# An attention and channel-mix kernel: the older rows are mixed into a buffer of their own, and one relu moves a step on

## Chip, cores and metric

One Trainium2 chip (trn2), one core of it. The time is the device time of one execution in microseconds; the runs shown are three of the kernel before, with their median. A trace is of one further execution, taken by the hardware profiler.

## What is computed

The reference first runs attention over 8 batches of 12 heads, 448 rows each, 64 columns a head, all in fp32, with scores that are capped by a tanh:

```python
scores = cap * np.tanh(scale * np.matmul(q, k.transpose(0, 1, 3, 2)) / cap)
attn = softmax(scores)                      # with 1e-9 added to the sum
x = np.matmul(attn, v)                      # heads side by side: 448 rows x 768 columns a batch
x_prev = x shifted down by one row, with a row of zeros ahead
xk = mu_k * x + (1.0 - mu_k) * x_prev
xr = mu_r * x + (1.0 - mu_r) * x_prev
k = np.maximum(xk @ w_k, 0.0)               # 768 x 1024
out = sigmoid(xr @ w_r) * ((k * k) @ w_v)   # 768 x 768 and 1024 x 768
```

## The kernel before, in words

Two heads make a pair, six pairs a batch, 48 pairs in all. The kernel goes through steps: step i computes the scores of pair i and, in the same step, later work of the pairs before it. Columns of x stand on the partitions (128 for a pair, so that hp = i % 6 is the pair's place among the 768) and rows along the free dimension. fp32 products are made from three fp32r products each (high x high, low x high, high x low), so every operand is split into a high and a low part.

What one pair goes through, by the names in the code:

- Step i: `scores` (lines 277 and 270, S0 to S3) on TensorE into one of two pairs of PSUM banks, `tanh` (line 290) and `exp` (line 303) on ScalarE, `red` (line 339) on VectorE, which sums the rows in blocks.
- Step i+1: `values` (V or W, lines 314 and 330) on TensorE into `pv`, one PSUM bank from a pool of two, so that the values of pair i+2 take the bank of pair i. `gather` (line 345) is four small DMAs that bring the sums of the four partition quarters together; `recip` (lines 349 to 356) adds and inverts them on VectorE; `rec_store` (line 359) writes them to DRAM; `rec_load` (line 368) reads them back, spread over the partitions, once they have landed.
- Step i+2: `norm` (line 372) multiplies `pv` by them into x on VectorE. `mix_old` (line 382) on ScalarE computes (1 - mu_k) times the row before. Before the change it writes this over the pair's own `pv` bank. `mix_new` (line 387) on VectorE adds mu_k times the row itself and writes `xk`. So the bank is in use until mix_new is done, and the values of pair i+2, in step i+3, wait for it. `x_high` and `x_low` (GpSimd, xkh and xkl) split xk; `gate_old` (line 405, GpSimd) and `gate_new` (line 399, VectorE) do the same mixing with mu_r, from SBUF alone.
- When a batch has its six pairs, its key matmuls (`K`, `krow` line 489 or `kpart` line 464, 144 positions a batch) are spread over the next batch's steps. They fill two PSUM banks; a bank that is finished goes on the list `done`, and `relu` (line 501, ScalarE) reads whatever stands on that list at this point of the program. `k_store` (ScalarE's queue) or `k_put` (SyncE's queue) writes it to DRAM. `turn` (line 496) is a tiny ScalarE copy out of a key bank that holds back the key matmuls behind it.

After step 49 the second phase follows (line 702): the two big products by a seven-product scheme, solid on TensorE.

The order of the work is written out by hand. A step's list of names is a string: `STEP_0`, `STEP_6`, `STEP_7`, `EVEN_6`, `ODD_6` for steps 0 to 11, `TURN` for 12 and 13, and for steps 14 to 47 `ROWS`, of which `rows(phase)` picks those names whose prefix holds the phase (i % 6), with the matmuls' part put in for `PE`, `PE_TURN` and `PE_END`; steps 48 and 49 have `LAST`. Each engine executes its own instructions in the order of the program. In phase 5 (steps 17, 23, 29, 35, 41, 47) the matmuls `S2 N0 K18` stand ahead of `tanh1 exp1 relu` in the program; N0 is the first scores of the next step's pair. K18 finishes no block there, except in step 47: the keys of batch 6 go over to the plain order at position 108 (`ROWS_LAST`), so its last 18 finish block 6 of batch 6, and the relu of that step has three blocks to read instead of two. The lines that set this:

```python
        self.xold = self.PV.pop(i)[:, 0:S]                     # 381, mix_old
        self.nc.scalar.mul(self.xold, self.X[i % 2][:, 0:S], self.om["k"][:, hp:hp + 1])
            self.PV[i] = self.ps_v.tile([P, 512], F32, name="pv")   # values; the pool has two
        for b, fc, ps in self.done:                            # relu
```

Of the kernel before, what the change touches and what calls it, by code (L numbers as in the profile page):

```python
# [10 lines left out]
F32 = mybir.dt.float32  # L11
# [6 lines left out]
B, H, S, D = 8, 12, 448, 64  # L18
# [6 lines left out]
NPAIR = B * NP  # L25
# [4 lines left out]
P = 128  # L30
# [28 lines left out]
ODD = """load_v gather quad_load weight_load S0 S1 V S2 red3 f f f f f gate_new tanh0 exp0 red0  # L59
# [2 lines left out]
weight_abs load_qk rec_load quad_load tail_open weight_store"""  # L62
EVEN = ODD.replace("V S2", "V S3 S2").replace(" red3", "").replace("tanh2", "tanh3 tanh2").replace("K relu k_store prep\n", "K exp3 red3 relu k_store prep\n")
ROWS = """load_v gather quad_load weight_load PE 135:red3 f f f f f gate_new tanh0 exp0 5:PE_TURN red0
weight_sum tanh1 exp1 14:PE_TURN 25:relu red1 norm recip x_store 14:k_put rec_store 25:k_put qk_high qk_low 2:mix_old 024:tanh3 tanh2 03:exp2 3:relu 01345:mix_old 0:relu mix_new x_high x_low gate_old
1245:exp2 red2 weight_rest weight_sum 024:exp3 024:red3 weight_abs load_qk rec_load quad_load weight_store PE_END"""
ROWS_PE = (("S1 V S3 S2 K18", "", "N0 N1 K15"), ("V", "turn S2 K15", ""), ("S0 S1 W K6 T S3 S2 K18", "", ""),
           ("S0 S1 V S2 K18", "", "N0 N1 K12"), ("V S3", "turn S2 K18", ""), ("S0 S1 V", "turn K6 S2 N0 K18", ""))
STEP_0 = """gather rec_load load_v x_store weight_load S0 S1 V0 S2 V1 S3 V2 V3 f f f f f tanh0 exp0 red0
weight_sum tanh1 exp1 weight_abs red1 recip rec_store qk_high qk_low tanh2 exp2 norm red2 tanh3 exp3 mix_old red3 mix_new x_high x_low  # L70
load_qk weight_store"""
ODD_6 = """load_v gather weight_load weight_low S0 S1 V S2 red3 f f f f f gate_new tanh0 exp0 red0 norm
weight_sum tanh1 exp1 K relu_early red1 tanh2 qk_rise relu exp2 mix_old k_store mix_new recip x_store rec_store qk_low x_high x_low gate_old
K red2 weight_rest weight_sum relu k_store K K weight_abs relu k_store load_qk rec_load weight_store"""
EVEN_6 = ODD_6.replace("V S2", "V S3 S2").replace(" red3", "").replace("tanh2 qk_rise", "tanh3 tanh2 qk_high").replace("weight_abs", "weight_abs exp3 red3")
# [6 lines left out]
TURN = (EVEN_6.replace("K K weight_abs", "K relu k_store weight_abs") + " N0 N1 K15",  # L82
        " ".join(x for x in ODD_6.replace("S0 S1 V S2", "V").replace("exp1", "exp1 turn S2 K15").split() if x not in ("K", "relu", "relu_early", "k_store")))
LAST = """gather f f f f V recip rec_store norm rec_load K mix_old relu k_store prep mix_new x_high x_low gate_old
K gate_new relu k_store prep K prep K relu k_store prep x_store tail_open"""
ALONE = 8
ROWS_LAST = 6 * NF * ND * 3 + 108


def rows(phase):  # L90
    pe = dict(zip(("PE", "PE_TURN", "PE_END"), ROWS_PE[phase]))
    do = [x.split(":") for x in ROWS.split()]
    return " ".join(pe.get(x[-1], x[-1]) for x in do if len(x) == 1 or str(phase) in x[0])


def strings(i):
    if i < ALONE:
        return ((STEP_0, STEP_0) if i < 6 else (STEP_6, STEP_7))[i % 2]
    if i < REST[0]:
        return (TURN if i >= 12 else (EVEN_6, ODD_6))[i % 2]  # L100
    if i < NPAIR:
        return rows(i % NP)
    return ((LAST, LAST) if i < NPAIR + 2 else (EVEN, ODD))[i % 2]


def f(ap):
# [3 lines left out]
class Body:  # L110
# [170 lines left out]
    def left(self, i):  # L281
        return (i,) if i < ALONE else (i, i + 1)

    def left_slots(self, i):
        return slice(i % 2, i % 2 + 1) if i < ALONE else slice(0, 2)

# [87 lines left out]
    def mix_old(self, i):  # L374
        b, hp = i // NP, i % NP
        if hp == 0:
            xh = self.xkp[b % 2].tile([P, ND, S], F32R, name="xkh", tag="xkh")
            xl = self.xkp[b % 2].tile([P, ND, S], F32R, name="xkl", tag="xkl")
            self.XK[b] = (xh, xl)

        self.xold = self.PV.pop(i)[:, 0:S]
        self.nc.scalar.mul(self.xold, self.X[i % 2][:, 0:S], self.om["k"][:, hp:hp + 1])

    def mix_new(self, i):
# [58 lines left out]
    def kpart(self, n0, n1):  # L443

        nc, per = self.nc, NF * ND * 3
        for n in range(n0, n1):
            b, r = divmod(n, per)
            if per <= n < ROWS_LAST:
                self.krow(b, r)
# [377 lines left out]
    def step(self, i, KS):  # L827

        nq = 0
        if self.maxima and i < NPAIR and i % 2 == 0:  # L830
            for j in (i, i + 1):
                self.row_maxima(j)
        pair = dict(load_qk=i + (3 if i < ALONE else 4), qk_high=i + 2, qk_low=i + 2, qk_rise=i + 2, load_v=i, S=i, tanh=i, exp=i, red=i)
        pair.update(dict.fromkeys("V W T gather recip rec_store".split(), i - 1))
        pair.update(dict.fromkeys("norm mix_old mix_new x_high x_low gate_old".split(), i - 2))
        pair.update(x_store=i - 3, gate_new=i - 3, N=i + 1)
        for op in strings(i).split():
            if op[0] == "K":
                n = self.k_next
# [11 lines left out]
            if op in pair:  # L851
                j = pair[op] if j is None else j
                if op == "load_qk" and i == ALONE:
                    self.load_qk(ALONE + 3)
                if i == NPAIR + 1 and op in ("x_high", "x_low"):
# [211 lines left out]
```

## Time and profile before

| | |
|---|---|
| runs, median (lowest to highest) | 906.75 us (906.21 to 907.01) |
| the profiled execution | 908.35 us |
| its span, first to last instruction | 906.5 us |
| TensorE (PE) busy | 874.6 us, 96% |
| VectorE (DVE) busy | 728.0 us, 80% |
| ScalarE (ACT) busy | 626.5 us, 69% |
| GpSimd (POOL) busy | 411.7 us, 45% |
| mean granted TensorE clock | 0.993 |
| the chain that ended last, by engine | PE 49%, DVE 25%, DMA 11%, ACT 5%, SPq 4% |

A line of the profile names the engine, the line of the kernel, the operation and its tiles as out<-in. SPq is SyncE's DMA queue, PEld the loading of weights. "[1.42 <-DVE xk L387]" behind an instruction says that its engine stood idle for 1.42 us before it, until the instruction of VectorE at line 387 that writes xk ended. PEclk is the granted share of the full TensorE clock: 1.00 is 2.4 GHz, 0.50 is 1.2 GHz. Matmuls follow one another in a pipeline, so a matmul's printed time overlaps the next one's. "x12" in a timeline is the number of instructions merged into one line.

### The profile page before, as it was taken

What the parts mean: (1) busy time and instruction counts of PE and PEld (TensorE: products, weight loads), DVE (VectorE), ACT (ScalarE), POOL (GpSimd) and SP (SyncE); (2) the same over time, 40 slices, a digit from 0 to 9 for tenths busy, and PEclk for the clock granted to TensorE, in tenths of its full rate; (3) what the DMA queues carried; (4) which work ended last, traced back from release to release, by engine and by line L of the source; (5) the groups of instructions that cost most, each with busy time, mean ns of one, the idle gap of its engine ahead of it and who ended that gap; (6) DMA issues with size and microseconds to landing.
All of it is one profiled execution on the core that took longest, in us unless ns stands there. A gap on an engine that the chain in (4) does not pass through costs nothing.

```text
span 906.5 us, 16778 instructions
## 1 busy us (share of the span) xinstructions
PE 874.6 (96%) x5826; PEld 705.4 (78%) x5826; DVE 728.0 (80%) x1246; ACT 626.5 (69%) x925; POOL 411.7 (45%) x345
## 2 busy tenths in 40 slices
PE   7889999999999999999999899999999999999997
PEld 3236666776667677766766699999999999999996
DVE  6888995988988899889868756887887667777775
ACT  8998887877788777878876365656565535555553
POOL 5996574777777777767763200000000024444330
PEclk9999999999999999999999999999999999999999
DMA  5465746677666776667565455745445546677663
GB/s 166 158 217 177 222 143 188 181 203 215 186 208 194 213 211 194 205 205 215 172 192 183 153 187 175 245 146 170 151 155 165 172 148 185 219 219 223 213 220 115
DMA packets 123679, 170.15 MB, mean 188 GB/s; under 512 B 22592, under 2 KB 107712, under 8 KB 123584
## 3 DMA queue, kind: packets, MB, share of 16 engines
q1 hardware_dynamic: 120992, 164.88, 59.4%
q10 hardware_dynamic: 2592, 4.10, 1.2%
q8 instruction: 48, 0.79, 0.4%
q14 instruction: 47, 0.39, 0.1%
HBM read 109.91 MB, written 56.60 MB: 184 GB/s over the span
## 4 chain that ended last, share of the span: by engine, by line
PE 49%; DVE 25%; DMA 11%; ACT 5%; SPq 4%; issue 3%; POOL 0%; DVEq 0%; ACTq 0%; POOLq 0%
PE ps L702 39%; DVE r L339 8%; DMA sq__195<-r 8%; PE kps L464 4%; SPq L345 4%; ACT p L290 2%; DVE wsq L568 2%; DVE wa L571 2%; DVE xk L387 2%; PE pv L314 2%; DVE wa L573 2%; ACT p L303 2%; DVE sq__195 L349 2%; DMA r<-rec_d 2%; PE s L277 1%
## 5 line engine op out<-in xcount | busy, mean ns | idle before, releaser
L290 ACT ACTIVATE p<-s,scl_t 128x896 f32<-128x896 f32 (+1 forms) x172 | 166.4, 979 | 31.6 <-PE s L270 17.4
L339 DVE TRANSPOSE_TENSOR_REDUCE r<-p 128x28 f32<-128x896 f32 (+1 forms) x192 | 180.2, 968 | 9.5 <-ACT p L303 9.0
L303 ACT ACTIVATE p<-p,cap_t 128x896 f32<-128x896 f32 (+1 forms) x172 | 175.0, 1024 | 4.6 <-ACT ko L501 0.4
L314 PE MATMUL pv<-p,rv 128*64 128x448 f32 x576 | 125.7, 565 | 18.6 <-DVE xk L387 18.4
L666 POOL TENSOR_TENSOR s<-src 128x384 f32<-128x384 f32 x14 | 14.3, 1021 | 266.4 <-DVE lo L687 266.4
L702 PE MATMUL ps<-wvh,hi 128*128 128x384 f32 x392 | 131.0, 334 | 0.0
L702 PE MATMUL ps<-wvl,hi 128*128 128x384 f32 x392 | 131.0, 334 | 0.0
L686 ACT CAST hi<-s 128x512 fp32r<-128x512 f32 (+1 forms) x112 | 63.6, 568 | 89.5 <-PE ps L702 76.8
L687 DVE TENSOR_TENSOR lo<-s,hi 128x512 fp32r<-128x512 f32 (+1 forms) x112 | 70.0, 625 | 59.2 <-ACT hi L686 43.4
L489 PE MATMUL kps<-xkh,wkh 64*128 64x448 f32 (+1 forms) x540 | 113.8, 369 | 0.0
L489 PE MATMUL kps<-xkh,wkl 64*128 64x448 f32 (+1 forms) x540 | 112.2, 362 | 0.0
L489 PE MATMUL kps<-xkl,wkh 64*128 64x448 f32 (+1 forms) x540 | 112.0, 362 | 0.0
L134 POOL TENSOR_TENSOR qkl<-rqk,qkh 128x896 fp32r<-128x896 f32 x47 | 100.5, 2139 | 10.2 <-ACT qkh L128 6.7
L314 PEld LDWEIGHTS pv<-p,rv 128*64 128x64 f32 x576 | 36.7, 138 | 81.6 <-issue 47.9
L702 PE MATMUL ps<-wrh,hi 128*128 128x384 f32 x294 | 98.9, 336 | 0.3 <-DVE o L725 0.3
L702 PE MATMUL ps<-wrl,hi 128*128 128x384 f32 x294 | 98.8, 336 | 0.0
L686 ACT CAST hi<-src 128x512 fp32r<-128x512 f32 (+1 forms) x84 | 47.7, 568 | 62.9 <-PE ps L702 59.9
L702 PE MATMUL ps<-wvh,lo 128*128 128x384 f32 x392 | 83.7, 334 | 0.0
L584 POOL TENSOR_TENSOR wsq<-wa,wsq 128x384 f32<-128x384 f32 (+1 forms) x40 | 54.2, 1354 | 60.7 <-DVE wsq L577 48.5
L687 DVE TENSOR_TENSOR lo<-src,hi 128x512 fp32r<-128x512 f32 (+1 forms) x84 | 56.8, 676 | 21.5 <-ACT hi L686 19.3
L702 PEld LDWEIGHTS ps<-wvh,hi 128*128 128x128 f32 x392 | 73.6, 188 | 0.1
L702 PEld LDWEIGHTS ps<-wvl,hi 128*128 128x128 f32 x392 | 73.6, 188 | 0.0
(118 smaller groups left out, 1920.3 us busy)
## 6 DMA issues: line engine op xcount, KB each, us to landing
rqk<-qk SPq DMA_DIRECT2D x47, 448.0 KB
src<-k_d SPq DMA_DIRECT2D x56, 256.0 KB
rv<-v SPq DMA_DIRECT2D x48, 256.0 KB
r<-rec_d SPq DMA_DIRECT2D x96, 112.0 KB
v_d<-o SPq DMA_DIRECT2D x56, 192.0 KB
src<-x_d SPq DMA_DIRECT2D x42, 256.0 KB
vl<-v_d SPq DMA_DIRECT2D x56, 192.0 KB
out<-o SPq DMA_DIRECT2D x55, 192.0 KB
```

The source lines that it names most:

```text
L134: {"p": self.nc.gpsimd, "v": self.nc.vector}[e].tensor_sub(*a)
L290: self.nc.scalar.activation(p32[:, n], self.S.pop((i, g))[:, n, 0:S], AF.Tanh, scale=self.scl_t)
L303: self.nc.scalar.activation(p32, p32, AF.Exp, scale=1.0 if self.maxima else self.cap_t)
L314: nc.tensor.matmul(pv[p, 0:S], v[:, g, h, :], ph[:, (h + i) % 2, :], start=(g == 0), stop=False)
L339: self.nc.vector.tensor_reduce(out=r1[:, 0:RM].rearrange("p (x g) -> p x g", g=3)[:, :, g] if g < 3 else r1[:, RM:RC], in_=p32.rearrange(" ...
L345: self.nc.sync.dma_start(self.sq[:, q % 2 * 2 + q // 2], self.r1[i % 2][32 * q:32 * q + 32])
L464: nc.tensor.matmul(self.kps[fc][:, 0:S], w, m[:, dc, :], start=first, stop=last)
L489: self.nc.tensor.matmul(self.kps[c][:, 0:S], w[p, dc, c * P:(c + 1) * P], m[p, dc, :], start=s == 0, stop=last or way == 2 and t == 2, ski ...
L584: {"p": self.nc.gpsimd, "v": self.nc.vector}[e].tensor_add(sq, f(a), sq)
L686: self.nc.scalar.copy(hi, x)
L687: self.nc.vector.tensor_sub(lo, x, f(hi))
L702: self.nc.tensor.matmul(o, a[:, c, :], w[:, c, :], start=first and k == 0, stop=last and k == len(todo) - 1, skip_group_check=True)
```

## The change

From pair 12 on (`ROWS_FIRST`), mix_old writes into a tile of its own in SBUF (`xold`, one buffer) instead of the pair's PSUM bank, so that the last reader of the bank is norm. In phase 5, the matmuls `S2 N0 K18` move in the program from behind `turn K6` to behind that step's relu; they stand in a new place called `PE_REST`. The relu of phase 5 so finds the two blocks that K6 finished on its list, and in step 47 the third block is left for a relu and a store that are put at the head of step 48.

```diff
-weight_sum tanh1 exp1 14:PE_TURN 25:relu red1 norm recip x_store 14:k_put rec_store 25:k_put qk_high qk_low 2:mix_old 024:tanh3 tanh2 03:exp2 3:relu 01345:mix_old 0:relu mix_new x_high x_low gate_old
-1245:exp2 red2 weight_rest weight_sum 024:exp3 024:red3 weight_abs load_qk rec_load quad_load weight_store PE_END"""
+weight_sum tanh1 exp1 14:PE_TURN 25:relu 5:PE_REST red1 norm recip x_store 14:k_put rec_store 25:k_put qk_high qk_low 2:mix_old 024:tanh3 tanh2 03:exp2 3:relu 01345:mix_old 0:relu mix_new x_high x_low gate_old
+1245:exp2 red2 weight_rest weight_sum 024:exp3 024:red3 weight_abs load_qk rec_load quad_load weight_store 03:PE_END"""
...
-           ("S0 S1 V S2 K18", "", "N0 N1 K12"), ("V S3", "turn S2 K18", ""), ("S0 S1 V", "turn K6 S2 N0 K18", ""))
+           ("S0 S1 V S2 K18", "", "N0 N1 K12"), ("V S3", "turn S2 K18", ""), ("S0 S1 V", "turn K6", "S2 N0 K18"))
...
+ROWS_FIRST = 12
...
-    pe = dict(zip(("PE", "PE_TURN", "PE_END"), ROWS_PE[phase]))
+    pe = dict(zip(("PE", "PE_TURN", "PE_REST" if phase == 5 else "PE_END"), ROWS_PE[phase]))
...
-    return ((LAST, LAST) if i < NPAIR + 2 else (EVEN, ODD))[i % 2]
+    return (("relu k_store " + LAST, LAST) if i < NPAIR + 2 else (EVEN, ODD))[i % 2]
...
         self.xold = self.PV.pop(i)[:, 0:S]
+        if i >= ROWS_FIRST:
+            self.xold = self.up.tile([P, S], F32, name="xold", bufs=1)
         self.nc.scalar.mul(self.xold, self.X[i % 2][:, 0:S], self.om["k"][:, hp:hp + 1])
```

## Rows read from the trace of the kernel before

**Rows 1.** Windows: length, busy PE, PEld, DVE, ACT, POOL, PEclk, DMA share, GB/s

```profile
155.00:480.00 325.00, 318.55 (x2639) 227.02 (x2637) 283.72 (x479) 264.27 (x336) 233.01 (x183) 1.00 0.68 201
...
505.00:545.00 40.00, 40.00 (x194) 33.89 (x191) 26.44 (x37) 21.98 (x36) 5.04 (x4) 0.96 0.53 175
545.00:907.00 362.00, 354.81 (x2046) 354.10 (x2044) 270.54 (x490) 194.92 (x377) 60.05 (x56) 1.00 0.58 182
```

**Rows 2.** Waits of PE, 155 to 505 us: total, times, longest

```profile
PE pv L314 <- DVE xk L387: 11.0, 12, 2.8
```

**Rows 3.** Waits of DVE, 155 to 505 us

```profile
DVE sq__195 L349 <- DMA sq__195<-r: 26.1, 26, 2.0
...
DVE r L339 <- ACT p L303: 4.9, 5, 1.7
```

**Rows 4.** Timeline of SyncE's queue: two rec_store, one step apart

```profile
302.91 0.33 SPq L359 DMA_DIRECT2D rec_d<-rs  x1
...
313.47 0.34 SPq L359 DMA_DIRECT2D rec_d<-rs  x1
```

**Rows 5.** Timeline of ACT in steps 47 and 48: start, us, engine, line

```profile
490.36 0.64 ACT L382 ACTIVATE pv<-x,om_k 128x448 f32<-128x448 f32 x1 [2.72 <-DVE x L372]
...
494.76 0.14 ACT L496 COPY turned<-kps 128x1 f32<-128x1 f32 x1
...
496.80 0.96 ACT L501 ACTIVATE ko<-kps 128x448 f32<-128x448 f32 x2
501.32 0.54 ACT L501 ACTIVATE ko<-kps 128x448 f32<-128x448 f32 x1 [3.56 <-PE kps L464]
...
503.20 1.04 ACT L303 ACTIVATE p<-p,cap_t 128x896 f32<-128x896 f32 x1
511.67 0.64 ACT L382 ACTIVATE pv<-x,om_k 128x448 f32<-128x448 f32 x1 [7.42 <-DVE x L372]
```

**Rows 6.** Timeline of DVE: norm, mix_new of pair 45; mix_new 46; xkl 47

```profile
498.62 0.58 DVE L372 TENSOR_TENSOR x<-pv,r 128x448 f32<-128x448 f32 x1
...
503.32 0.68 DVE L387 SCALAR_TENSOR_TENSOR xk<-x,mu_k,pv 128x448 f32<-128x448 f32 x1 [1.81 <-ACT pv L382]
...
512.41 0.68 DVE L387 SCALAR_TENSOR_TENSOR xk<-x,mu_k,pv 128x448 f32<-128x448 f32 x1 [0.78 <-ACT pv L382]
...
520.53 0.63 DVE L134 TENSOR_TENSOR xkl<-xk,xkh 128x448 fp32r<-128x448 f32 x1 [0.63 <-ACT xkh L128]
```

**Rows 7.** Timeline of PE: values of pair 46, last keys, values of pair 47

```profile
492.75 2.48 PE L314 MATMUL pv<-p,rv 128*64 128x448 f32 x12 [1.42 <-DVE xk L387]
...
497.38 0.47 PE L464 MATMUL kps<-xkh,wkh 128*128 128x448 f32 x1
...
504.05 4.17 PE L314 MATMUL pv<-p,rv 128*64 128x448 f32 x12 [2.77 <-DVE xk L387]
```

**Rows 8.** Windows around the two waits of rows 7, columns as rows 1

```profile
490.00:497.00 7.00, 5.58 (x44) 3.27 (x40) 5.32 (x11) 6.58 (x9) 3.10 (x3) 1.00 0.46 156
...
505.00:506.00 1.00, 1.00 (x6) 0.44 (x4) 1.00 (x2) 0.00 (x0) 1.00 (x2) 0.50 0.48 158
```

**Rows 9.** Lines 387, 399, 382, 426 by themselves: ns least/median/most

```profile
L387 DVE SCALAR_TENSOR_TENSOR xk<-x,mu_k,pv x48: 626/627/682, 31.5 to 519.2; 128x448 f32<-128x448 f32 x48
...
L399 DVE SCALAR_TENSOR_TENSOR xg<-x,mu_r,xg x34: 661/679/1347, 160.0 to 513.0; 128x448 f32<-128x448 f32 x34
...
L382 ACT ACTIVATE pv<-x,om_k x48: 618/639/643, 30.1 to 518.5; 128x448 f32<-128x448 f32 x48
...
L426 ACT ACTIVATE xl<-xo,om_r x14: 657/659/672, 547.3 to 713.2; 128x448 f32<-128x448 f32 x14
```

**Rows 10.** Timeline of PE: first keys of the last batch on pairs 46, 47

```profile
517.77 0.37 PE L464 MATMUL kps<-xkh,wkh 128*128 128x448 f32 x1
...
523.97 0.37 PE L464 MATMUL kps<-xkh,wkh 128*128 128x448 f32 x1
```

**Rows 11.** Waits of POOL, 155 to 505 us

```profile
POOL xkh L124 <- DVE xk L387: 71.6, 34, 8.1
```

More of the change, by code (lines that the diff above doesn't have):

```diff
@@ L99, in strings @@
     if i < REST[0]:
-        return (TURN if i >= 12 else (EVEN_6, ODD_6))[i % 2]
+        return (TURN if i >= ROWS_FIRST else (EVEN_6, ODD_6))[i % 2]
     if i < NPAIR:
         return rows(i % NP)
-    return ((LAST, LAST) if i < NPAIR + 2 else (EVEN, ODD))[i % 2]
+    return (("relu k_store " + LAST, LAST) if i < NPAIR + 2 else (EVEN, ODD))[i % 2]
 def f(ap):
```

## The prediction, made before the changed kernel ran

> **What bounds the kernel now.** I read the busy times by stretch first. From 155 to 480 us, the steady steps of attention, TensorE is busy 318.55 of 325 us at full clock, so it looks like the bound; from 505 to 545 it has no gap at all, and behind that it is busy for 354.81 of the 361.5 us left, the last outputs included [rows 1]. Then the waits: between 155 and 505 us TensorE stood idle for one reason only, the values' matmuls waiting for mix_new: 12 times, 11.0 us [rows 2]. That wait is what the change takes away, and the naive sum is 11 us.
>
> So the next question is what sets the pace of mix_new. The waits of VectorE in the same stretch name no TensorE instruction: 26 waits, 26.1 us, are for the gather's DMA and 5, 4.9 us, for an exp [rows 3]. The queue of SyncE shows why: rec_store is issued at 302.91 and the next one at 313.47, 10.56 us later, about one step, and in between the queue runs rec_store, rec_load (which waits for rec_store to land), a few other transfers, the gather, and then recip waits for the gather to land [rows 4]. This ring (recip, rec_store, rec_load, gather, recip) has no matmul in it. The stretch of 350 us holds 350 / 10.56 = 33 such rounds, and mix_new, right behind recip in VectorE's order, keeps their pace. TensorE is about 11.0 / 33 = 0.33 us a step faster than the ring, and the wait on mix_new is where it gives that back. Freed at norm, the bank lets TensorE run ahead of the ring, but only once: norm of a pair stands between recip of the pair before and the two reductions in VectorE's order, so it has the ring's pace too. What TensorE gains in the steady steps it will lose again in front of norm, of tanh's banks or of the `turn`. I therefore count a gain only where TensorE ends a stretch that nothing else limits: in steps 47 and 48, after which TensorE is solid, so that what it gains there reaches the end [rows 1].
>
> **Steps 47 and 48, part by part.** In step 47 ScalarE's order is two relus, a third relu, tanh2, mix_old of pair 45, exp2. The third relu reads the key block that the step's last 18 key matmuls finish: ScalarE stands still for 3.56 us before it, until 501.32 [rows 5]. Only then come tanh2, mix_old and mix_new, for which VectorE waits 1.81 us, until 503.32 [rows 6]. The values of pair 47, first in step 48, need the bank of pair 45, so they start at 504.05, after 2.77 us idle: the key matmuls before them ended at 501.28 [rows 7]. After that wait the granted clock is 0.50, the lower level (1.2 GHz); in 490 to 497 it is 1.00 [rows 8]. These 12 matmuls take 4.17 us, the same 12 of pair 46 take 2.48: 1.69 us more [rows 7].
>
> The change takes both causes away. The bank of pair 45 is free when norm ends, 498.62 + 0.58 = 499.20 [rows 6], 2.1 us before TensorE wants it at 501.28. The relu of the third block moves behind exp2; then tanh2 runs at 497.8 (behind the two relus, 496.80 + 0.96), mix_old at 499.2 (norm's end) for 0.64 us and exp2 for 1.04 us, to about 500.9 [rows 5], so the third part of the values, which starts some 1.6 us into them, finds its operand. **Gain: 2.77 us of idle and 1.69 us of slow clock, 4.46 us**, if the 18 key matmuls end when they do now. They will: the first waits for the first relu of step 47 (ready at 496.80 + 0.54, start 497.38), which ScalarE reaches by mix_old of pair 44 at 490.36, after a wait for norm of 2.72 us, and then exp, tanh and `turn` in a row [rows 5, 7]. That is the ring again, so nothing upstream of it moves them.
>
> The other edits. **Order of step 17, 23, ... 47:** the matmuls of `S2 N0 K18` keep their order on TensorE, and the relus before them keep theirs on ScalarE; only the list that relu works off changes, and only in step 47 are there three blocks. Cost nothing in the other steps. In step 47 SyncE puts two key blocks instead of three, and in step 48 ScalarE issues one more relu (0.54 us) and one store, where it waits 7.42 us for norm anyway [rows 5].
>
> **mix_new from SBUF:** with a PSUM input it takes 627 ns, the same operation with two SBUF inputs (the gate's mix) 679 ns in the median [rows 9]. Below, the price is nothing; above, 1347 - 627 = 720 ns, the longest of those rows. I take 52 ns, since the median is of the same shape and in the same steps. It lies beside the DMA wait in 26 steps and on the ring in 33 - 26 = 7: 0.36 us. **mix_old into SBUF:** 659 against 639 ns for the same form [rows 9], on the path only where VectorE waits for an exp that follows mix_old, 5 times [rows 3]: 0.10 us. Its new buffer is single, but the mix_new that empties it lies a step back.
>
> **What is late next:** the key matmuls of the last batch. Those that need pair 46 start at 517.77, those that need pair 47 at 523.97 [rows 10]. Shifted by 4.46 us that is 513.31 and 519.51. mix_new of pair 46 ends at 512.41 + 0.68 = 513.09, xkl of pair 47 at 520.53 + 0.63 = 521.16 [rows 6]. Their chain moves by up to 1.81 us, what mix_new of pair 45 no longer waits: that leaves 2.0 us for xkh and xkl of pair 46, and xkl of pair 47 is ready at 519.35, so nothing waits. If the chain did not move, xkl of pair 47, which the third matmul reads (two spacings of 0.2 us later, 519.92), would be 1.24 us late. Between 0 and 1.24, I take 0.2, since the wait that held the chain goes altogether.
>
> **Sum:** -4.46 + 0.36 + 0.10 + 0.20 = -3.80 us. The profiled execution took 908.35 us, 1.85 more than its span of 906.5; it becomes 904.55. It stands 1.60 us over the median of the runs, 906.75, so against those the forecast is 902.95 us. About 0.2% of the time, 1.8 us, is what a measurement of this kernel tells from no change.
>
> **Rivals.**
> *The idle time moves and takes the clock along* (17%). The values of pair 46 wait 1.42 us now and start at 492.75 [rows 7]. Freed at norm of pair 44 (just before mix_old, 490.36) they start some 2.4 us sooner and end near 492.8, but the key matmuls behind them wait for `turn`, which ends at 494.90 [rows 5]: about 2.1 us idle in one piece. After 1.42 us the clock held, after 2.77 us it fell [rows 7, 8]; 2.1 lies between. If it falls, some 1.2 of such 1.69 us are lost, as about 0.5 us of room lies before the 18 key matmuls: 904.1.
> *The values of pair 47 find another wait* (11%): their third part at exp2 (about 500.9), or their load. A part of the 2.77 us stays and the clock falls all the same: on average 1.4 us gained, 905.4.
> *TensorE was the bound after all* (9%). All 11.0 us come back [rows 2], with 1.69 of clock: 906.75 - 12.7 = 894.1. For it speaks that no other wait of TensorE is listed; against it, that VectorE waits for DMA 26 times and never for a matmul [rows 3].
> *Slower, by a port* (6%). mix_new gets its second input from SBUF while GpSimd reads there. Its rows of two SBUF inputs reach 1347 ns [rows 9], so a third of the steps at that price is 0.24 us a step, 33 x 0.24 = 7.9 on the ring: 906.75 + 7.9 - 4.5 = 910.2. It decides from 4.46 / 33 = 0.14 us a step. Against it: GpSimd stands idle before each xkh, 34 waits of 2.1 us in the mean, and what it waits for is mix_new itself [rows 11], so it hardly reads at that moment. The Trainium skill ("SBUF — State Buffer", Who interferes with whom) says that a VectorE instruction with two SBUF inputs contends with a GpSimd instruction that reads SBUF, while one with at most one SBUF input does not: by that rule this change moves mix_new into the contending kind. The long rows agree with it; no run before shows mix_new itself in that form.
> *The change doesn't free the bank at norm* (3%), and the values go on waiting for mix_new. With the relu gone from its way mix_new of pair 45 runs 1.81 us sooner [rows 6], and the values of pair 47 with it; 2.77 - 1.81 = 0.96 us stays idle, less than the 1.42 after which the clock held [rows 7, 8]: 1.81 + 1.69 - 0.66 of costs = 2.84 us gained, 903.9.
>
> **How the numbers follow.** The forecast has 54%; its own range is 902.0 to 903.9. Faster are the forecast, the moved idle time, the full gain and the bank that isn't freed: 0.54 + 0.17 + 0.09 + 0.03 = 0.83. Within 0.2% is the other wait: 0.11. Slower is the port: 0.06. The range goes from 900.5 (a ring that comes out 2 us quicker, as its DMA waits are not fixed) to 905.8, which takes in most of the case with another wait: 0.54 + 0.17 + 0.03 and most of 0.11, about 0.8.
>
> **What would show it.** Right: no wait of a value matmul on mix_new from pair 14 on, few on norm; ScalarE's third relu of step 47 behind exp2 without a wait of microseconds; the values of pair 47 directly behind the key matmuls, in 2.5 us at full clock; but rec_store to rec_store still about 10.5 us, so that mix_old of pair 44 comes within 1 us of 490.36 [rows 5] and TensorE's idle time in the steady steps stands before other instructions. Wrong: mix_old of pair 44 earlier by several us (then TensorE set the ring's pace), a mix_new of 1 us or more, or a stretch at the lower clock in step 47.

## The result, and the profile after

The changed kernel is slower: 911.5 us in the median of 12 runs against 906.38 of the kernel before beside it, ratio 1.0053, 95% interval 1.0028 to 1.0078, or +4.8 us (2.5 to 7.1). A second set of runs gave 1.0039 (1.0019 to 1.0058), +3.5 us. Single runs of either kernel lie up to 8.7 us apart, much wider than the three first shown, so times below are ratios to runs of the kernel before in the same set, given in us, and one profile alone settles nothing below some 3 us (an estimate from that spread). The profiled execution took 912.58 us with a span of 910.8.

Windows of the changed kernel, columns as in [rows 1]:

```profile
155.00:480.00 325.00, 321.36 (x2615) 223.11 (x2612) 283.75 (x480) 261.44 (x332) 231.33 (x183) 1.00 0.68 199
480.00:505.00 25.00, 23.03 (x178) 16.23 (x175) 20.43 (x29) 17.83 (x24) 8.80 (x7) 0.93 0.60 180
505.00:545.00 40.00, 38.45 (x190) 32.27 (x189) 27.65 (x37) 21.54 (x35) 6.51 (x5) 1.00 0.58 190
```

TensorE is busier in the steady steps than before (321.36 of 325 us against 318.55) and yet the trace counts fewer matmuls there (2615 against 2639). From 480 to 505 us its granted clock is 0.93, and from 505 to 545, where it had no gap, 1.55 us are idle. Its waits from 155 to 510 us:

```profile
PE kps L492 <- POOL xkl L135: 2.2, 6, 0.6
PE kps L492 <- ACT turned L499: 2.0, 1, 2.0
PE kps L492 <- ACT ko L504: 0.5, 1, 0.5
PE kps L492 <- POOL xkh L125: 0.3, 1, 0.3
```

The 11.0 us of waits on mix_new [rows 2] are gone, so the change does what it says. In their place stand short waits on GpSimd's xkl and ScalarE's relus, and one of 2.0 us on `turn`. VectorE waits for the gather as before, 26.4 us in 22 pieces against 26.1 in 26 [rows 3]. Its wait for the reciprocals from DRAM (r), 0.2 us in one piece before, is 1.4 us in three; that for xg was there before (6.0 us in 4):

```profile
DVE sq__195 L350 <- DMA sq__195<-r: 26.4, 22, 1.9
DVE r L340 <- ACT p L304: 6.1, 6, 1.7
DVE xg L402 <- POOL xg L408: 5.6, 4, 2.3
DVE x L373 <- DMA r<-rec_d: 1.4, 3, 0.6
```

The two mixes by themselves (ns least/median/most), which answer to [rows 9]:

```profile
L390 DVE SCALAR_TENSOR_TENSOR xk<-x,mu_k,xold x36: 629/631/684, 156.8 to 524.3; 128x448 f32<-128x448 f32 x36
...
L385 ACT ACTIVATE xold<-x,om_k x36: 659/670/673, 154.7 to 523.5; 128x448 f32<-128x448 f32 x36
```

In the median mix_new costs 4 ns more than from PSUM, mix_old 31 ns. Step 47 on TensorE (values of pair 46, then the 6 key matmuls, then the 18):

```profile
496.03 2.60 PE L315 MATMUL pv<-p,rv 128*64 128x448 f32 x12
500.60 0.74 PE L492 MATMUL kps<-xkh,wkh 64*128 64x448 f32 x2 [1.97 <-ACT turned L499]
501.14 0.57 PE L492 MATMUL kps<-xkh,wkl 64*128 64x448 f32 x2
...
508.00 1.35 PE L315 MATMUL pv<-p,rv 128*64 128x448 f32 x6
```

The values of pair 47 (508.00) stand directly behind the keys, as forecast; but 1.97 us of idle came up ahead of the 6 keys, and behind it a pair of matmuls takes 0.57 us where the same pairs took 0.36 or 0.37 before:

```profile
495.46 0.37 PE L489 MATMUL kps<-xkh,wkl 64*128 64x448 f32 x2
495.67 0.36 PE L489 MATMUL kps<-xkl,wkh 64*128 64x448 f32 x2
```

Three stretches part the loss. Up to norm of pair 12, which the change doesn't touch, the changed kernel took 154.00 us against 151.22; kernels with that same part took 150.8 to 155.6 in the profiles below, so this is spread. From norm of pair 12 to norm of pair 44 ("the steady stretch") it took 341.4 against 338.5 us, from there to the end of the span 415.4 against 416.8.

### The profile page after: what moved, and what is told of

It reads as the page before. It is cut to its first block, busy times and chain, and to the rows that moved or that the text cites. A ratio compares the mean times of both kernels' runs of the same rounds, so it can differ in the third digit from the quotient of the medians.

```text
span 910.8 us, 16779 instructions
## 1 busy us (share of the span) xinstructions
PE 879.0 (97%) x5826; PEld 704.7 (77%) x5826; DVE 730.6 (80%) x1246; ACT 626.4 (69%) x925; POOL 411.4 (45%) x345
## 4 chain that ended last, share of the span: by engine, by line
PE 49%; DVE 23%; DMA 12%; SPq 6%; ACT 4%; issue 3%; POOL 1%; DVEq 0%; POOLq 0%; ACTq 0%
PE ps L705 39%; DVE r L340 7%; DMA sq__195<-r 7%; SPq L346 5%; PE kps L467 4%; DMA r<-rec_d 3%; PE pv L315 2%; PE kps L492 2%; DVE xk L390 2%; DVE wsq L571 2%; DVE wa L574 2%; DVE sq__195 L350 2%; PE s L278 2%; DVE wa L576 2%; ACT p L291 2%
## 5 line engine op out<-in xcount | busy, mean ns | idle before, releaser
L492 PE MATMUL kps<-xkh,wkh 64*128 64x448 f32 (+1 forms) x540 | 116.9, 372 | 2.9 <-ACT turned L499 2.0
L492 PE MATMUL kps<-xkl,wkh 64*128 64x448 f32 (+1 forms) x540 | 114.2, 365 | 2.2 <-POOL xkl L135 2.2
L492 PE MATMUL kps<-xkh,wkl 64*128 64x448 f32 (+1 forms) x540 | 114.2, 364 | 0.0
L492 PEld LDWEIGHTS kps<-xkh,wkh 64*128 64x128 f32 (+1 forms) x540 | 64.0, 185 | 17.9 <-ACT turned L499 6.5
```

The source lines that it names most:

```text
L492: self.nc.tensor.matmul(self.kps[c][:, 0:S], w[p, dc, c * P:(c + 1) * P], m[p, dc, :], start=s == 0, stop=last or way == 2 and t == 2, ski ...
```

## The experiments

**The parts.** First each half of the change alone, the change for the last pairs alone, and the new tile alone:

```diff
# rows_only: the change, but steps 47 and 48 ordered as before (relu move undone)
# relu_only: the change without
-        if i >= ROWS_FIRST:
-            self.xold = self.up.tile([P, S], F32, name="xold", bufs=1)
# late_old:  if i >= 45:      tile_last: rows_only with  if i >= 47:
# rows_mid:  rows_only with  if 12 <= i < 44:
# all_but_44: the change with  if i >= 12 and i != 44:
```

> The changed kernel with the move of the third key block's relu undone: older rows mixed into SBUF from pair 12 on, steps 47 and 48 ordered as before. Theory U (using the SBUF rows lets TensorE run ahead and makes the steady steps 12 to 44 slower): the stretch from the first normalising that the change touches (pair 12) to that of pair 44 is 2 to 4 us longer than before, the first 150 us are as before within 1 us, and the time is +2 to +4 us. Theory P (the new tile moves the other tiles, whatever it is used for): the first 150 us are 2 to 3 us longer already and the time is +4 to +5 us. Theory N (the two profiles differ by chance): the time is within 1 us of before.

> The changed kernel with the older rows mixed into the values' PSUM bank for every pair, as before; only the relu of step 47's third key block is read in step 48. No new tile. Theories U and P: nothing is lost in steps 0 to 44; the idle of 2.8 us before the values of pair 47 shrinks since mix_old of pair 45 no longer stands behind three relus, so -2 to -4 us. Rival (the turn's relus bind step 47 wherever the third one stands): -1 to +1 us.

> The changed kernel, but the older rows go to SBUF only from pair 45 on; the relu is moved as in the change. Theory U: steps 12 to 44 are as before, TensorE is not ahead before the 6 key matmuls of step 47, so the whole forecast of the end comes, -2.5 to -4.5 us. Theory P: the tile is there, so the first 150 us are 2 to 3 us longer, and the time is 0 to -2 us. Theory N: -3 to -5 us, as the changed kernel would have it on average.

> The kernel before with the SBUF tile for older rows used by the last pair (47) alone, where nothing waits for the bank; no other edit. It has the layout of SBUF of the changed kernel and the order of before. Theory P: +2 to +5 us. Theories U and N: within 1 us of before.

| kernel | ratio to before (95%) | us | steady stretch, us |
|---|---|---|---|
| before (profile) | | | 338.5 |
| rows_only | 1.0031 (1.0008 to 1.0055) | +2.8 | 335.0 |
| relu_only | 0.9972 (0.9951 to 0.9994) | -2.5 | 334.3 |
| late_old | 0.9975 (0.9955 to 0.9995) | -2.3 | 333.9 |
| tile_last | 1.0003 (0.9985 to 1.0020) | +0.3 | 336.5 |

The tile alone costs nothing that can be measured (+0.3 us, -1.4 to 1.8), so theory P falls; theory N falls with it, since rows_only and relu_only differ from before by more than their intervals allow for chance. Theory U has the time of rows_only right, but not its profile, whose steady stretch is shorter than before's. The relu's move gains about what the end could give; late_old shows how, and what is lost again. Its TensorE in step 48 and the last batch's keys:

```profile
501.07 2.48 PE L316 MATMUL pv<-p,rv 128*64 128x448 f32 x12
...
511.75 0.47 PE L468 MATMUL kps<-xkh,wkh 128*128 128x448 f32 x1 [0.97 <-ACT ko L505]
```

and ScalarE, on which those keys wait:

```profile
510.60 0.67 ACT L386 ACTIVATE xold<-x,om_k 128x448 f32<-128x448 f32 x1 [8.87 <-DVE x L374]
511.17 0.52 ACT L505 ACTIVATE ko<-kps 128x448 f32<-128x448 f32 x1
...
519.16 2.31 ACT L821 CAST wvh<-w 128x768 fp32r<-128x768 f32 x3
521.37 1.57 ACT L821 CAST wvh<-wsq 128x768 fp32r<-128x768 f32 x2
522.84 1.57 ACT L821 CAST wvh<-w 128x768 fp32r<-128x768 f32 x2
524.31 0.83 ACT L821 CAST wvh<-wvl 128x768 fp32r<-128x768 f32 x1
525.04 0.98 ACT L505 ACTIVATE ko<-kps 128x448 f32<-128x448 f32 x2
```

The 12 value matmuls of pair 47 take 2.48 us behind the keys with no idle: the whole 4.46 us of the forecast. But the next key blocks need banks that a relu empties. One relu stands behind mix_old of pair 46, which waits 8.87 us for norm; the next behind eight casts of weights. TensorE, now earlier, waits 0.97 and 1.04 us for them; from 505 to 545 us it waits for nothing else:

```profile
PE kps L468 <- ACT ko L505: 2.0, 2, 1.0
```

From the values of pair 46 to the end of the span late_old takes 904.0 - 492.71 = 411.3 us, before 906.5 - 492.75 = 413.75: 2.45 us gained, 4.46 less these 2.01.

The rows of pairs 12 to 43 remained as the cost, and three more runs tested that:

> The changed kernel once more, unedited. Theory A (the two parts add up: rows +2.3 to +2.9 us, relu -2.3 to -2.5 us, as each alone measured): 0 to +1 us against the kernel before. Theory I (together they cost more than their sum, as the first twelve runs have it): +4 to +6 us.

> The kernel before with the older rows in SBUF for pairs 12 to 43 alone; pairs 44 to 47 and the relus as before, so the end has the order and the waits of before. Theory S (the cost of the rows lies in the steady steps): +2 to +3 us. Theory E (it lies in steps 45 to 48, where TensorE comes early to the 6 key matmuls and waits 2 us for the turn's copy): 0, within 1 us.

> The changed kernel with pair 44 alone mixed into its bank, so that the values of pair 46 wait for mix_new of pair 44 as before and TensorE is not early at the 6 key matmuls of step 47. Theory E: no wait for the turn's copy, no stretch of half clock in 480 to 505 us, rec_store of pair 44 to that of pair 47 29.4 us as in the kernel with the relu's move alone, and the time is 1 to 2 us below the changed kernel, -2 to -3 us against before if the rest is free. Theory S: the same at the end, but the steady steps cost 2 to 3 us: 0 to +1 us against before. Theory I: within 1 us of the changed kernel.

Measured: after_again 1.0039, +3.5 us; rows_mid 1.0040 (1.0022 to 1.0058), +3.6 us; all_but_44 1.0053 (1.0026 to 1.0080), +4.8 us. rows_mid has the end of the kernel before, so theory E falls and a loss of that size lies in the steady steps. all_but_44 took the wait for `turn` in step 47 away (0.2 us left from 480 to 505 us, granted clock 1.00 there) and gained nothing measurable, where theory S had 0 to +1 us against before. Theory A falls too: the rows alone (+2.8 or +3.6 us) and the end alone (-2.3 or -2.5 us) would make +0.3 to +1.3 us together, and the whole measured +3.5 (1.7 to 5.3) and +4.8. No run shows where the rest, some 3 us with an interval as wide, arises. The steady stretch is 335.0 to 342.9 us in the five profiles with rows in SBUF (mean 340.0) and 333.9 to 338.5 in the four without (mean 335.8): 4.2 us.

**Where in the steady steps.** I compared the five by the step's place in its cycle of six. The pairs 16, 22, 28, 34, 40 stand out. SyncE's queue there, changed kernel, pair 16:

```profile
188.82 0.34 SPq L360 DMA_DIRECT2D rec_d<-rs  x1
189.25 0.79 SPq L517 DMA_DIRECT2D k_d<-ko  x2
190.13 1.53 SPq L207 DMA_DIRECT2D rqk<-qk  x1
192.46 1.12 SPq L369 DMA_DIRECT2D r<-rec_d  x2
```

and before:

```profile
186.01 0.34 SPq L359 DMA_DIRECT2D rec_d<-rs  x1
186.44 0.79 SPq L514 DMA_DIRECT2D k_d<-ko  x2
187.33 0.41 SPq L206 DMA_DIRECT2D rqk<-qk  x1
187.83 2.08 SPq L368 DMA_DIRECT2D r<-rec_d  x2
```

In both one DMA's issue lasts some 1 us too long. Before, it is the second load of reciprocals; after, the load of queries ahead of them, so rec_load follows rec_store by 3.64 us instead of 1.82; 1.1 us of the difference is the issue, 0.7 a wait of SyncE until rec_store has landed. Over the five pairs the mean from rec_store to rec_load is 1.82 to 1.97 us in the four profiles without rows and 2.49 to 3.35 with them. What holds SyncE up shows in the DMA view of those microseconds (190.0 to 191.3 after):

```profile
q8 instruction: 1, 0.02, 6.0%
```

It is a fetch of instructions. Before, the whole stretch from 155 to 490 us has 22 of them, 16.4 KB each:

```profile
q8 instruction: 22, 0.36, 0.5%
```

At 20 of these 22 a DMA issue of SyncE lasts 0.5 to 1.1 us longer than its like. It holds the other way round as well: of SyncE's 419 DMA issues in this stretch 21 last over 0.4 us longer than the median of their kind, and 20 of them meet one of the 22 fetches (the other, at 463.46, meets a fetch of 8 KB on a second instruction queue, q14). Between the first and the last, 21 gaps, the trace has 5,373 instructions of TensorE, 5,312 of them matmuls and weight loads: 256 a gap in the mean. No other engine has more than 643 there. So it is TensorE's program that is fetched, one block every 256 instructions or 1.5 steps. The Trainium skill ("Runtime: NRT & Kernel Launch", Instruction fetch mechanics) states the same blocks of 16 KiB, 256 instructions, and calls their cost mostly hidden; for TensorE the trace agrees, since its waits from 155 to 505 us, 11.0 us, are all for mix_new [rows 2]; for SyncE's queue the measurement decides: 0.5 to 1.1 us at 20 of 22 fetches.

**Moving the fetch.** That made theory F: what counts is where in the ring's step the fetch falls. Matmuls of one column, put in steps 3 to 10 where TensorE waits anyway, shift all later fetches and nothing else that I know of:

```diff
+        for _ in range(PAD // 8 + (i - 3 < PAD % 8) if g == 1 and 3 <= i < 11 else 0):
+            nc.tensor.matmul(s[0:1, 0, S + 32:S + 33], self.mu["k"][:, 0:1], self.mu["k"][:, 0:1], start=True, stop=True)
         if g == 2:
             self.QK.pop(i)
```

> The kernel before with 12 one-column matmuls more (24 instructions of TensorE) in steps 3 to 10, into unused columns of a score bank; nothing else. Theory F (a fetch of TensorE's code, 16 KB about every 256 of its instructions, holds up SP's DMA issue for about 1 us, and what counts is where in the step it falls): every later fetch falls 24 instructions, some 1.2 us, earlier in the step, so that of steps 16, 22, 28, 34, 40 falls on the key stores or the load of queries ahead of rec_load, as in the changed kernel; rec_store to rec_load of these pairs goes from 1.9 to about 2.8 us and the time to +2 to +4 us. Theory R (it is TensorE's running ahead or the SBUF operand itself): within 1 us of before.

> The changed kernel with 112 such matmuls (224 instructions) in steps 3 to 10: every later fetch falls 32 instructions, some 1.6 us, later in the step. Theory F: the fetch of steps 16, 22, 28, 34, 40 falls on or behind rec_load, rec_store to rec_load there goes from 2.9 back to 1.9 us, and the time to between -1 and +2 us against before, 2 to 4 us below the changed kernel. Theory R: +4 us against before, as the changed kernel.

> The changed kernel with 32 such matmuls (64 instructions): every later fetch falls some 3.3 us earlier. Theory F: the fetch of steps 16, 22, 28, 34, 40 falls where SP waits for the reciprocals and holds up nothing there, rec_store to rec_load 1.9 us; the fetches of the steps between move to just ahead of a gather, where they may hold it up: -3 to +1 us against the changed kernel. Theory R: as the changed kernel, within 1 us.

> The kernel with the relu's move alone (-2.5 us) and the 112 matmuls. Theory F: the fetches fall 1.6 us later, that of steps 16, 22, 28, 34, 40 behind rec_load and ahead of the next gather, -1 to -4 us against before. Theory R: -2.5 us, as without them.

> The changed kernel with 56 one-column matmuls. The trace of the run before showed that each counts four instructions of TensorE (two loads, two matmuls), so these are 224, and every later fetch falls 32 instructions, some 1.6 us, later: that of steps 16, 22, 28, 34, 40 from 6.4-7.4 us behind the gather to 8-9 us, where the kernel before has it (7.3-8.1) or a little behind. Theory F: rec_store to rec_load of these pairs 1.9 us, the stretch from the normalising of pair 12 to that of pair 44 within 334 to 338 us as in the kernels that keep the bank, -2 to +1 us against before. Theory R (the loss is not the fetch's): +4 us.

> The kernel before with 6 such matmuls, 24 instructions, so that every later fetch falls 1.2 us earlier, the fetch of those five steps at 6.1-6.9 us behind the gather, where the changed kernel has it. Theory F: rec_store to rec_load of these pairs 2.6 to 3 us and +2 to +5 us against before. Theory R: within 1 us of before.

Each such matmul turned out to be two loads and two matmuls, so the first four shifted twice as far as meant. Measured: before_pad12 +5.3 us (3.3 to 7.4), after_pad112 +1.1 (-0.5 to 2.6), after_pad32 +4.2 (2.8 to 5.6), relu_pad112 +0.8 (-0.9 to 2.6) against -2.5 without, after_pad56 +3.1 (1.4 to 4.9), before_pad6 +1.2 (-0.4 to 2.7). The nine kernels with added matmuls, of this part and the next, reach norm of pair 12 after 150.6 to 152.9 us, no later than those without, so the matmuls by themselves cost no time that shows. The same 112 matmuls make one kernel faster and another slower, which theory R has no place for. But of F's ranges only that of after_pad112 held clearly: before_pad12, relu_pad112 and after_pad56 came out above theirs, before_pad6 below, and after_pad32 fits both theories. The detail, too, came out otherwise than F had it: in before_pad6 the fetch of the five steps did not move (7.5 to 8.2 us behind the gather in four of them, as before), and after_pad56 and after_pad32 had rec_load back at 1.8 us and lost elsewhere, in the steps whose gather or rec_store now met a fetch. A fetch put ahead of rec_load is at most one place that costs, not the only one. The next run bears on this:

```diff
-... weight_abs load_qk rec_load quad_load ...
+... weight_abs 01234:load_qk rec_load 5:load_qk quad_load ...
```

> The changed kernel with the load of queries behind rec_load in the steps of phase 5 (those that bring back the reciprocals of pairs 16, 22, 28, 34, 40); the fetch stays where it is in TensorE's program. Theory F: a fetch that fell on the load of queries no longer holds up rec_load, rec_store to rec_load of these pairs from 2.9 to 1.8-2.3 us; what it then holds up is the next gather, so 0.5 to 2.5 us below the changed kernel. Theory R: as the changed kernel, within 1 us.

1.0079 (1.0054 to 1.0105), +7.1 us: rec_store to rec_load fell to 1.96 us as expected, and the time did not fall (the changed kernel had +4.8 and +3.5 us). Those five rounds of the ring got longer (11.56 us from rec_store to the next against 10.99 in the mean of the kernels with rows), because from the next gather to its reciprocals 6.19 us went by instead of 5.42. The load of queries now stands between rec_load and that gather; that it is what holds the gather up is not shown.

**The operand, the running ahead, and four positions.** The last four runs part the causes. rows_held is rows_mid with one more instruction: the rows of pairs 12 to 43 lie in SBUF, but VectorE clears a column of the bank behind mix_new, so TensorE waits as before:

```diff
+        if self.held is not None:
+            self.nc.vector.memset(self.held[:, 0:1], 0.0)
```

> The kernel before with the older rows in SBUF for pairs 12 to 43, but the values' bank held as before: VectorE clears one column of it (128x1) right behind mix_new, so the next values wait for that. Theory F (TensorE running ahead moves its fetches and small waits against the ring of reciprocals): rec_store to rec_load of pairs 16, 22, 28, 34, 40 1.8 to 2.0 us as before, and the time 0 to +2.5 us, what is above 0 being the 32 clearings. Theory O (the SBUF operand itself slows the steady steps): as with the bank freed, +3.6 us and the clearings on top, +4 to +6 us.

> The kernel before with 32 one-column matmuls in steps 3 to 10 (128 instructions of TensorE): the partner of the changed kernel with the same 32. Theory F (the change costs by where the fetches fall; with the fetches moved it costs another amount, of either sign): this one lies anywhere from -3 to +6 us against before, so that the changed kernel less this one is not +4 us in each of the four pairs (0, 32, 56, 112 matmuls) and lies within 2 us of 0 in the mean. Theory S (rows in SBUF cost 3 to 4 us in the steady steps wherever the fetches fall): this one is within 1.5 us of before, and the changed kernel 3 to 5 us above it.

> The kernel before with 56 such matmuls (224 instructions): partner of the changed kernel with 56. Theories F and S as for 32: F -3 to +6 us against before, S within 1.5 us of before.

> The kernel before with 112 such matmuls (448 instructions): partner of the changed kernel with 112 (+1 us against before). Theory F: +1 to +5 us against before (the relu's move alone lost 3 us by these 112). Theory S: -3 to -1 us, that is 3 to 4 us below the changed kernel with 112.

rows_held: 0.9997 (0.9980 to 1.0013), -0.3 us; rec_store to rec_load of the five pairs 1.83 us. TensorE waits for the cleared column, and the clearings are short:

```profile
PE pv L315 <- DVE pv L394: 3.1, 5, 0.8
PE pv L315 <- DVE xk L391: 2.8, 1, 2.8
```

```profile
L394 DVE MEMSET pv<- 128x1 f32 x32 | 1.9, 59 | 0.0
```

So the operand in SBUF costs nothing that can be measured; theory O falls. What costs 3.6 us in rows_mid is the freed bank alone, that is TensorE running ahead. And whether the change costs depends on the matmuls added, that is on where the fetches fall if F is right:

| matmuls added | before | changed | difference |
|---|---|---|---|
| 0 | 0 | +4.8, +3.5 | +4.1 |
| 32 | +6.8 (4.5 to 9.2) | +4.2 | -2.6 |
| 56 | +8.0 (5.2 to 10.9) | +3.1 | -4.9 |
| 112 | +4.2 (2.6 to 5.8) | +1.1 | -3.1 |

(us against the kernel before as it is; each from its own ratio. From the intervals, the differences with matmuls are known to about 2.7, 3.3 and 2.2 us, an estimate, so that of 32 is just not told apart from nothing.) With matmuls added the change gains 2.6 to 4.9 us; as the kernel stands, it loses 4.1. The mean of the four is -1.6, within F's 2 us of 0. Theory S of these runs falls: it had the kernel before within 1.5 us of itself with 32 and 56 matmuls. F had these two at no more than +6 us, and they came out above. The profile of before_pad56 is of its fastest run (905.67 us), so no trace shows where its 8.0 us go.

The gain isn't the rows'. With 112 matmuls the relu's move alone stands 3.4 us below the kernel before (+0.8 against +4.2) and the rows on top of it add 0.3 (+1.1); with 32 and 56 the two were not measured apart. So the freed bank costs some 4 us as the kernel stands and nothing that can be measured with 112 matmuls, and no pair shows that it gains. With none added the kernel before is at the fastest of the six positions tried (0, 6, 12, 32, 56 and 112 matmuls; 6 not told apart from 0).

## Why the prediction was wrong

*Steady steps: no gain, +0.46 us of costs.* Right that the 11.0 us are no reserve: no steady stretch got below 333.0 us in any of the kernels, and mix_old of pair 44 came 5.6 us later in the changed kernel's profile, not sooner (2.8 us of it from before pair 12). Right too, and too high, on mix_new's price (4 ns in the median, not 52) and near on mix_old's (31 ns, not 20). Wrong was the step "a gain only where TensorE ends a stretch that nothing else limits", with running ahead counted at nothing: it let TensorE gain or hold, never lose. In its place the runs showed that running ahead is an edit of its own. With the bank freed the steady steps cost some 4 us (rows_mid +3.6, steady stretch +4.2), and with the same operand but the bank held nothing (rows_held -0.3). What carries that cost is shown in part: TensorE's place against SyncE's queue shifts, and with it the fetches that hold that queue up. The trace of before had the sign of it, and my working left it out: 22 fetches in the DMA view, and at 298.85 a DMA issue of SyncE of 1.40 us whose like took 0.53 at 310.64, while I took the ring's pace from one round [rows 4].

*Steps 47 and 48: -4.46 us.* The mechanism was right, and late_old shows it: values of pair 47 behind the keys without idle, in the 2.48 us of full clock. In the changed kernel's profile the end, from norm of pair 44 on, gained 1.3 us. *What is late next*, +0.20 us, was the term mis-sized: it measured 2.01 us in late_old (1.4 us in the changed kernel). I followed xkh and xkl of the last pairs, but not the relus that empty the key banks; behind an engine said to be solid I had not asked which of its operands had time to spare only because it was late. The end alone is worth -2.3 to -2.5 us.

*The rivals.* "The idle time moves and takes the clock along" came true in the changed kernel: 1.97 us before the 6 keys, then matmuls at the lower clock (0.57 us a pair). Its price was small: all_but_44, without it, is no faster. That the values of pair 47 find another wait did not happen.

"Slower, by a port", the only one on the side where the result fell, came near the measured time by luck (+3.5 us forecast). Its mechanism is in the trace, but hardly any of the time. The Trainium skill ("SBUF — State Buffer", Who interferes with whom) has a VectorE instruction with two SBUF inputs contend with a GpSimd instruction that reads SBUF. The trace agrees: of the 36 executions of mix_new with both inputs in SBUF ten met GpSimd's splitting of the queries (qkl), and the seven that met it for 156 to 181 ns took 640 to 660 ns, the rest 629 to 632 ns but for the last two (683 and 684 ns, with no GpSimd beside them). Before, with one input in PSUM, seven met it for 159 to 178 ns and took 626 or 627 ns. One meeting of each, first in the changed kernel, then before:

```profile
378.47 2.14 POOL L135 TENSOR_TENSOR qkl<-rqk,qkh 128x896 fp32r<-128x896 f32 x1
380.43 0.66 DVE L390 SCALAR_TENSOR_TENSOR xk<-x,mu_k,xold 128x448 f32<-128x448 f32 x1
```

```profile
373.07 2.13 POOL L134 TENSOR_TENSOR qkl<-rqk,qkh 128x896 fp32r<-128x896 f32 x1
375.03 0.63 DVE L387 SCALAR_TENSOR_TENSOR xk<-x,mu_k,pv 128x448 f32<-128x448 f32 x1
```

Over the whole kernel that is under 0.2 us. The rival was wrong in how much of mix_new GpSimd meets: its rows of 1,340 to 1,347 ns had met it for 1.26 us each. rows_held, with the same operand, costs nothing that can be measured.

TensorE as the bound (-12.7 us) and a bank that isn't freed are refuted by the time and by the waits.

*Open.* That a fetch holds up SyncE is seen in the trace; that its place decides the change's sign is argued from the pairs, not shown: the matmuls in steps 3 to 10 shift all of TensorE's program, and I know of no other lasting effect. Which of the fetches costs how much isn't settled: the two runs aimed at the one ahead of rec_load (before_pad6, after_recfirst) did not confirm it as the whole loss. Nor were the short waits that came up as TensorE ran ahead (2.2 us on xkl) parted from it. A kernel with the gain and without the loss was among the runs: the relu's move alone, -2.5 us, beats both.

## What to carry to other kernels

An edit that takes a wait off an engine also moves everything that this engine does in time, and where another loop sets the pace, that can cost more than the wait was worth; try the edit with the freed engine held back (one cleared column), to part the edit from the running ahead. In a kernel of thousands of matmuls an effect of 0.5% should be measured at two or three shifts of the program (a few idle matmuls early on) before it is called the edit's. And behind a stretch that is to come sooner, list each operand that the engine takes next and how long before it is ready now.

## What the hardware showed that I had not expected

A fetch of 16 KB of TensorE's program made a DMA issue of SyncE last 0.5 to 1.1 us longer at 20 of 22 places, though the DMA engines were busy for only 0.68 of the time in the steady steps. Twelve to 112 matmuls that compute nothing, in steps where TensorE waits, made the kernel before slower by 4.2 to 8.0 us, though the stretch that holds them grew by nothing that shows.
